# A fused RWKV attention and MLP-mixer kernel: the second down weight in two issues, one batch turned by DMA, two loads held, the last step in two halves of columns

## The chip, the cores and the metric

The kernel runs on one core of one Trainium2 chip. The metric is the device time of one execution in microseconds (us), the median of several runs. The engines are named as in the profile: PE (TensorE, matrix products), DVE (VectorE), ACT (ScalarE), POOL (GpSimd) and SP (SyncE, which here only issues DMAs). PEld is the loading of weights into PE, which overlaps its products.

## The reference

Two stages follow each other. The first is a recurrent attention over 768 positions, for 4 batches of 8 heads of 48 elements; the second is a token mixer and a channel MLP on rows of 384 elements (8 heads times 48).

```python
for t in range(S):                                  # stage 1, per batch and head
    cur = einsum('bhd,bhe->bhde', u * k[t], v[t])
    y[t] = einsum('bhd,bhde->bhe', r[t], state + cur)
    state = w * state + einsum('bhd,bhe->bhde', k[t], v[t])
x = y, heads side by side                           # 4 x 768 x 384
h = (relu(x.T @ w_tok1) @ w_tok2).T                 # token mixing, 768 -> 256 -> 768
u = x + h
out = u + relu(u @ w_ch1) @ w_ch2                   # channel MLP, 384 -> 1536 -> 384
```

## The kernel before

**Units.** The recurrence is computed in chunks of 128 positions. There are 4 batches of 6 chunks, so 24 units, numbered 0 to 23; batch `b` has units `6b` to `6b+5`. A unit loads its rows of k, r and v (three DMAs, tiles `ld_k`, `ld_r`, `ld_v`), scales k and r by powers of the decay (steps `kp`, `rp`, tile `kpr`), casts v (`vb`), turns k and r so that the head's elements lie on the partitions (units 0 to 13 by PE, steps `trk`, `trr`, tile `tr_ps`, copied to `rk`; units 14 to 23 by a DMA transpose `t` straight into `rk`), forms the 128x128 products of each head (`at`, tile `at_ps`), masks them (`AT`), multiplies by v (`y`, tile `y_ps`, with the carried state by `yS`), updates the state (`kv`, `S`) and writes `x_b` (`x`).

**Batches.** When the six chunks of a batch are there, PE computes the token mixer: `hid` (two products for each chunk, `h_ps<-x_b,wtok`), its relu `hr` (tile `h1r`), and `bk`, one step for each chunk (`hT_ps`). DVE adds `x_b` and gives `u_sb` (step `us`, one for each chunk). `u_sb` has to be turned before the channel MLP. Before the change batches 0, 1 and 2 are turned by PE: step `tu` is three transposes of 128x128 into `t_ps`, and ACT or DVE copies them to `uT`. Batch 3 is turned by two DMA transposes on SP's queue, one for each half of three chunks. Then come, for each half of a batch (`sg` 0 and 1), twelve up steps `z` (three products of 128x384 each, `z_ps<-uT,wch`), whose relu `zr` falls to ACT, and for each of its three chunks four down steps `h` (three products each, `h_ps<-wch,zr`). A step is named by batch, half or chunk, and number: `z2_0_0` is the first up step of the first half of batch 2, `h1_5_3` the last down step of chunk 5 of batch 1. The first half of the down steps of a chunk (numbers 0 and 1) reads rows 0 to 5 of twelve of the down weight, the other (2 and 3) rows 6 to 11. `os` adds `u_sb` and the down product on DVE (tile `osb`), and SP writes it out.

**Order.** The kernel holds no order written by hand. `graph` (line 151 on) describes the steps with durations, ranks and dependencies, `Plan.run` places them on the engines by a greedy list schedule, and the instructions are then recorded in the planned order of starts. On the chip each engine, and each DMA queue, works through its instructions in that order, so that one that waits holds up all behind it. Four PSUM buffers (tag `m`) are shared by `tr`, `hid`, `bk`, `tu`, `z` and `h`. All loads, DMA transposes and output writes go through SP's queue. The five weight transfers (which cast to bf16) are issued by POOL, after step `rp5`; the last is `wch2`, the whole down weight, 1152 KB in bf16.

**Names that the change touches.** `weight` in `graph` and in the kernel function issues the weights; the loop at the end of each unit and `load` hold back a unit's first load (`CFG["hold"]`); `pe_turn` names the batches turned by PE, `uTd` is the DMA transpose of half a batch; `parts` cuts the last chunk's down step, `h`, `os_` and `out_`, into halves of columns.

Of the kernel before, what the change touches and what calls it, by code (L numbers as in the profile page):

```python
# [27 lines left out]
NJ = 12  # L28
# [122 lines left out]
def graph(do, cfg):  # L151
# [50 lines left out]
    for u in range(NU):  # L202
# [81 lines left out]
    for b in range(B):  # L284
# [16 lines left out]
        for c in range(C if b not in direct else 0):  # L301
            bk = p.add(f"bk{b}_{c}", [("PE", 2 * MM, 2 * MM + 0.13)], hr + [wx[1]], take=True, rank=r + 0.01 * c, emit=do("bk", b, c))
            us = p.add(f"us{b}_{c}", [DVEP], [bk], give=[f"bk{b}_{c}"], rank=r, emit=do("us", b, c))
            if b in pe_turn:
                t = p.add(f"tu{b}_{c}", [("PE", 0.2, 0.4)], [us], take=True, rank=r + 0.01 * c + 0.005, emit=do("tu", b, c))
                uT.append(p.add(f"uT{b}_{c}", [("ACT", 0.36, 0.53), ("DVE", 0.26, 0.4)], [t], give=[f"tu{b}_{c}"], rank=r, emit=do("uT", b, c)))
            else:
                some.append(us)
                if c % G == G - 1:
                    s = p.add(f"i:uT{b}_{c}", [("SP", 1.35, 1.4)], some, rank=-3000 + c, emit=do("uTd", b, c // G))  # L310
                    uT += [p.transfer(f"x:uT{b}_{c}", s, 1.75, 2.4, 0.0)] * G
                    some = []
        for sg in range(2):
# [7 lines left out]
            for si in range(3):  # L321
# [3 lines left out]
                for part in range(parts):  # L325
                    h, n, mm = None, f"{b}_{c}" + "ab"[part] * (parts > 1), MM / parts + (0.005 if parts > 1 else 0.0)
                    for q in range(4):
                        x = 3 * mm + (own if q == 0 else 0.0)
                        h = p.add(f"h{n}_{q}", [("PE", x, x + 0.13)], zr[3 * q:3 * q + 3] + [wx[3], h], take=(q == 0), rank=m + 0.1 * sg + 0.05 + 0.01 * si + 0.001 * part - (0.02 if q else 0), emit=do("h", b, c, q, part, parts))
# [6 lines left out]
                    stores.append(p.transfer(f"x:o{n}", s, 0.63 / parts, 1.8, 0.0))  # L336
    last = None
# [3 lines left out]
    for s in p.steps:  # L341
        s.rank += cfg.get("rank", {}).get(s.name, 0.0)
# [26 lines left out]
def kernel(  # L369
# [155 lines left out]
    def load(eng, nm, i):  # L525
        b, c = divmod(i, C)
        t = lpool.tile([128, dm], f32, name=f"ld_{nm}")
        ins = sp.dma_start(h3(t), SRC[nm][b, :, ts(c, T), :].rearrange("h s d -> s h d"))
        if i in CFG.get("hold", {}) and nm == CFG.get("lorder", "krv")[0]:
            first = INS[CFG["hold"][i]]  # L530
            tc.add_manual_dep(ins.ins, first.ins.name,
                              mybir.DependencyInfo(mybir.DependencyClass.Sync, mybir.DependencyReason.DATA),
                              reason="weights first")
        loaded[nm, i] = t

    def weight(eng, i):
        t, src = [(wtok1, moe_w_tok1), (wtok2, moe_w_tok2), (wch1, moe_w_ch1), (wch2, moe_w_ch2), (wch1, moe_w_ch1)][i]
        cols = {2: slice(0, dch // 2), 4: slice(dch // 2, dch)}.get(i, slice(None))
        if i == 3 and CFG.get("runs"):
            for f in range(2):  # L540
                half = src[f * dch // 2:(f + 1) * dch // 2]
                pool.dma_start(t[:, f * NJ // 2:(f + 1) * NJ // 2, :], half.rearrange("(p c) k -> p c k", p=128))
        else:
            pool.dma_start(t[:, :, cols], src.rearrange("(c p) k -> p c k", p=128)[:, :, cols])
# [14 lines left out]
    def vb(eng, i):  # L559
        L[i]["vb"] = apool.tile([128, dm], bf16, name="vb")  # L560
        INS["vb", i] = act.copy(L[i]["vb"], loaded["v", i])
# [96 lines left out]
    def y(eng, i):  # L658
        y, first = y_ps(i)
        for a in range(HP):  # L660
            for q in range(2):
                h = 2 * a + q
                INS["y", i] = pe.matmul(y[:, ds(h * D, D)], L[i]["AT"][q][:, a, :], L[i]["vb"][:, ds(h * D, D)],
# [30 lines left out]
    def x(eng, i):  # L694
        b, c = divmod(i, C)
        dve.tensor_add(x_bs[b][:, c, :], L[i]["y"], L[i]["yd"])
# [19 lines left out]
    def bk(eng, b, c):  # L716
        M[b]["bk", c] = psM.tile([128, dm], f32, name="hT_ps", tag="m")
        for i in range(2):
            pe.matmul(M[b]["bk", c], wtok2[:, i, ts(c, 128)], M[b]["h1r"][:, i, :], start=(i == 0), stop=(i == 1))

    def us(eng, b, c):
        dve.tensor_add(M[b]["u"][:, c, :], x_bs[b][:, c, :], M[b]["bk", c])
# [33 lines left out]
    def wch1_j(m, j):  # L756

        if CFG.get("runs"):
            return wch1[:, m].rearrange("p (f q i) -> p f i q", f=2, i=NJ // 2)[:, j // 6, j % 6]
        return wch1[:, m, ts(j, 128)]  # L760

    def z(eng, b, sg, j):
# [3 lines left out]
        for m in range(3):  # L766
            pe.matmul(M[b]["z", sg, j].rearrange("p (c t) -> p c t", c=G), wch1_j(m, j), M[b]["uT"][:, sg * G:sg * G + G, m, :],
# [82 lines left out]
```

## Time and profile before

| | us |
|---|---|
| median of 3 runs | 167.95 |
| their range | 167.8 to 168.52 |
| the profiled execution's own time | 167.91 |
| span in its profile, first to last instruction | 166.2 |

The profile has five parts that are used below: the busy time of each engine, the span in 40 slices, the chain of waits (the chain of work that ended last, followed back from the last instruction), the groups of instructions, and the DMA issues. Beside the page, single views can be asked: the timeline (rows of start, duration, engine, operation, tiles and count, with the idle time before and what ended it in brackets), windows (busy time of every engine in given stretches), who waited for whom, one tile's instructions, and the DMA queues in a window. Matmuls are pipelined: a product of 384 columns has a duration of 326 ns, but the next starts about 163 ns after it.

### The profile page before, as it was taken

What the parts mean: (1) busy time and instruction counts of PE and PEld (TensorE: products, weight loads), DVE (VectorE), ACT (ScalarE), POOL (GpSimd) and SP (SyncE); (2) the same over time, 40 slices, a digit from 0 to 9 for tenths busy, and PEclk for the clock granted to TensorE, in tenths of its full rate; (3) what the DMA queues carried; (4) which work ended last, traced back from release to release, by engine and by line L of the source; (5) the groups of instructions that cost most, each with busy time, mean ns of one, the idle gap of its engine ahead of it and who ended that gap; (6) DMA issues with size and microseconds to landing.
All of it is one profiled execution on the core that took longest, in us unless ns stands there. A gap on an engine that the chain in (4) does not pass through costs nothing.

```text
span 166.2 us, 3805 instructions
## 1 busy us (share of the span) xinstructions
PE 157.5 (95%) x1475; PEld 99.7 (60%) x1475; DVE 100.9 (61%) x206; ACT 85.1 (51%) x172; POOL 80.4 (48%) x97
## 2 busy tenths in 40 slices
PE   6989899996999999999999999999999999999991
PEld 1567665653667666666665666666665565665650
DVE  5499897500288878995599789958967203021021
ACT  3994732797348536698434550457003923905800
POOL 7349680021548869989988789776300000000000
PEclk9999999999999999999999999999999999999999
DMA  5999999999999899998999997993121702102103
GB/s 106 219 224 206 128 147 201 191 184 199 185 216 255 172 221 213 258 205 159 225 210 218 203 190 152 223 239 77 32 99 47 142 0 97 51 0 95 47 29 113
DMA packets 94899, 25.67 MB, mean 154 GB/s; under 512 B 88353, under 2 KB 94882, under 8 KB 94882
## 3 DMA queue, kind: packets, MB, share of 16 engines
q1 hardware_dynamic: 91408, 22.29, 64.1%
q0 software_dynamic: 3472, 3.15, 12.2%
q8 instruction: 11, 0.18, 0.4%
q14 instruction: 6, 0.05, 0.1%
q10 hardware_dynamic: 2, 0.00, 0.0%
HBM read 20.65 MB, written 4.72 MB: 153 GB/s over the span
## 4 chain that ended last, share of the span: by engine, by line
PE 72%; DMA 13%; POOL 4%; ACT 3%; DVE 3%; issue 1%; SPq 1%; POOLq 0%; DVEq 0%; ACTq 0%
PE h_ps L411 30%; PE z_ps L411 21%; DMA wch<-in_moe_w_ch_dram 11%; PE at_ps L411 4%; PE y_ps L411 4%; PE hT_ps L411 4%; PE tr_ps L411 3%; PE kv_ps L411 3%; DMA ld_v<-in_v_dram 2%; ACT rk L411 2%; PE t_ps L411 1%; DVE rku L411 1%; POOL kpr L411 1%; POOL wch L411 1%; POOL yd L411 1%
## 5 line engine op out<-in xcount | busy, mean ns | idle before, releaser
L411 ACT ACTIVATE zr<-z_ps 128x384 bf16<-128x384 f32 x96 | 46.6, 492 | 38.9 <-PE z_ps L411 38.8
L411 PE MATMUL h_ps<-wch,zr 128*128 128x384 bf16 x288 | 55.1, 326 | 1.3 <-DMA wch<-in_moe_w_ch_dram 1.3
L411 PE MATMUL z_ps<-uT,wch 128*128 128x384 bf16 x288 | 53.0, 326 | 0.0
L411 DVE TENSOR_TENSOR osb<-u_sb,h_ps 128x384 f32<-128x384 bf16 x24 | 13.0, 549 | 42.5 <-PE h_ps L411 42.5
L411 PEld LDWEIGHTS <-wch 128*128 128x128 bf16 x288 | 27.2, 98 | 17.0 <-issue 0.2
L411 PEld LDWEIGHTS <-zr 128*128 128x128 bf16 x288 | 26.6, 98 | 17.0 <-DMA wch<-in_moe_w_ch_dram 1.7
L411 DVE TENSOR_TENSOR AT<-at_ps,mask 128x512 bf16<-128x512 f32 x48 | 31.2, 681 | 5.1 <-PE at_ps L411 5.0
L411 POOL TENSOR_TENSOR kpr<-ld_k,wn 128x384 bf16<-128x384 f32 x22 | 22.0, 1000 | 16.0 <-PE z_ps L411 11.4
L411 POOL TENSOR_TENSOR kpr<-ld_r,wp 128x384 bf16<-128x384 f32 x23 | 24.2, 1054 | 6.4 <-DMA ld_r<-in_r_dram 4.4
L411 POOL TENSOR_TENSOR yd<-vb,adg 128x384 f32<-128x384 bf16 x18 | 14.9, 831 | 15.3 <-DVE adg L411 9.5
L411 ACT COPY rk<-tr_ps 128x1024 bf16<-128x1024 bf16 x14 | 14.2, 1013 | 8.9 <-PE tr_ps L411 8.5
L411 PEld LDWEIGHTS <-kpr 128*128 128x128 bf16 x192 | 13.6, 107 | 5.3 <-DVE kpr L411 1.1
L411 DVE TENSOR_TENSOR x_b<-y_ps,yd 128x384 bf16<-128x384 f32 x24 | 13.2, 551 | 3.8 <-PE y_ps L411 3.5
L411 PEld LDWEIGHTS <-rk 48*128 48x128 bf16 (+1 forms) x272 | 10.7, 99 | 7.6 <-ACT rk L411 2.8
L411 ACT CAST vb<-ld_v 128x384 bf16<-128x384 f32 x24 | 12.3, 510 | 2.6 <-DMA ld_v<-in_v_dram 2.6
L411 PE MATMUL tr_ps<-ident,kpr 128*128 128x128 bf16 x112 | 12.3, 244 | 0.4 <-POOL kpr L411 0.2
L411 DVE TENSOR_TENSOR u_sb<-x_b,hT_ps 128x384 bf16<-128x384 bf16 x24 | 12.0, 547 | 1.0 <-PE hT_ps L411 1.0
L411 PE MATMUL h_ps<-x_b,wtok 128*128 128x384 bf16 x48 | 11.3, 326 | 0.1
L411 PE MATMUL at_ps<-rk 48*128 48x128 bf16 x192 | 10.2, 229 | 0.9 <-ACT rk L411 0.8
L411 PEld LDWEIGHTS <-AT 128*128 128x128 bf16 x192 | 8.3, 98 | 3.7 <-DVE AT L411 1.3
L411 PE MATMUL y_ps<-vb,AT 128*128 128x48 bf16 x192 | 9.8, 186 | 0.5 <-DVE AT L411 0.4
L411 PEld LDWEIGHTS <-wtok 128*128 128x128 bf16 x96 | 8.0, 97 | 3.6 <-issue 0.3
(66 smaller groups left out, 132.5 us busy)
## 6 DMA issues: line engine op xcount, KB each, us to landing
ld_k<-in_k_dram SPq DMA_DIRECT2D x24, 192.0 KB, 3.9
ld_r<-in_r_dram SPq DMA_DIRECT2D x24, 192.0 KB, 3.8
ld_v<-in_v_dram SPq DMA_DIRECT2D x24, 192.0 KB, 3.9
out_dram<-osb SPq DMA_DIRECT2D x24, 192.0 KB, 1.9
wch<-in_moe_w_ch_dram POOLq DMA_DIRECT2D x2, 576.0 KB, 9.4
wch<-in_moe_w_ch_dram POOLq DMA_DIRECT2D x1, 1152.0 KB, 18.0
wtok<-in_moe_w_tok_dram POOLq DMA_DIRECT2D x2, 384.0 KB, 5.4
u_bc<-in_u_dram SPq DMA_DIRECT2D x1, 192.0 KB, 4.4
```

Source lines behind the costliest of these rows:

```text
L411: return lambda *args, **kw: tc.keep_in_program_order(f(*args, **kw))
```

## The change

- The down weight `wch2` is fetched in two issues on POOL's queue, rows 0 to 5 (number 3) and then rows 6 to 11 (number 5). Down steps 0 and 1 wait for the first, 2 and 3 for the second.
- `pe_turn` loses batch 2: its 18 transposes on PE and six copies (five on DVE, one on ACT) go, and two DMA transposes on SP's queue take their place.
- The first load of unit 6 is held until the products `y5` are done (before: until the cast `vb5`). The first load of unit 21 is held until `us2_2`, the third sum of batch 2, is done (before: no hold).
- The last down step, chunk 5 of batch 3, is computed in two halves of 192 columns: 24 products of 192 columns instead of 12 of 384, two sums, two writes of 96 KB.
- Paths that no setting used (`runs`, `lorder`) are gone, and settings that stand unused (`xpe`, `off`) came in.

```diff
     def weight(i, after):
-        busy = 1.8 if i == 3 and cfg.get("runs") else 0.9
-        wi[i] = s = p.add(f"i:w{i}", [("POOL", busy, busy + 0.1, True)], after, rank=-50, emit=do("weight", i))
-        took = cfg.get("wtime", (3.0, 2.6, 3.1, 7.7, 3.1))[i]
+        wi[i] = s = p.add(f"i:w{i}", [("POOL", 0.9, 1.0, True)], after, rank=-50, emit=do("weight", i))
+        took = cfg.get("wtime", (3.0, 2.6, 3.1, 7.7, 3.1) if 5 not in cfg["wafter"] else (3.0, 2.6, 3.1, 3.9, 3.1, 3.9))[i]
...
-        for unit, (what, i) in cfg.get("hold", {}).items():
-            if i == u:
-                p.wait(gates[cfg.get("lorder", "krv")[0], unit], [dict(rp=rp, vb=vb, y=y)[what]])
...
-                        h = p.add(f"h{n}_{q}", [("PE", x, x + 0.13)], zr[3 * q:3 * q + 3] + [wx[3], h], take=(q == 0), rank=m + 0.1 * sg + 0.05 + 0.01 * si + 0.001 * part - (0.02 if q else 0), emit=do("h", b, c, q, part, parts))
+                        h = p.add(f"h{n}_{q}", [("PE", x, x + 0.13)], zr[3 * q:3 * q + 3] + [wx[3] if q < 2 else wx.get(5, wx[3]), h], take=(q == 0), rank=m + 0.1 * sg + 0.05 + 0.01 * si + 0.001 * part - (0.02 if q else 0), emit=do("h", b, c, q, part, parts))
...
+    for unit, what in cfg.get("hold", {}).items():
+        p.wait(gates["k", unit], [next(s for s in p.steps if s.name == "".join(map(str, what)))])
...
-    + [("w", 0), ("w", 1), ("w", 2), ("w", 4), ("w", 3)],
-    wafter={0: "x:v4", 1: "rp5", 2: "rp5", 4: "rp5", 3: "rp5"},
+    + [("w", 0), ("w", 1), ("w", 2), ("w", 4), ("w", 3), ("w", 5)],
+    wafter={0: "x:v4", 1: "rp5", 2: "rp5", 4: "rp5", 3: "rp5", 5: "rp5"},
     slack={"v5": 3.0},
-    hold={6: ("vb", 5)},
+    hold={6: ("y", 5), 21: ("us", "2_2")},
...
-    pe_turn=(0, 1, 2),
+    pe_turn=(0, 1),
...
+    parts=2,
...
+        rows = {3: slice(0, NJ // 2), 5: slice(NJ // 2, NJ)}.get(i, slice(None)) if 5 in CFG["wafter"] else slice(None)
+        pool.dma_start(t[:, rows, cols], src.rearrange("(c p) k -> p c k", p=128)[:, rows, cols])
```

Because the planner places everything anew, the order of instructions changes far from the edits too. Both programs, built, have these orders at the places that are spoken of below (steps of one engine, from left to right):

```text
PE, first down steps
  before  z0_0_0 ... z0_0_11, z0_1_0 ... z0_1_6, h0_0_0, h0_1_0, h0_0_1, h0_1_1, h0_0_2, ...
  after   z0_0_0 ... z0_0_11, h0_0_0, h0_1_0, h0_0_1, h0_1_1, h0_2_0, z0_1_0, h0_2_1, h0_0_2, ...
PE, batch 1 turned
  before  bk1_0, y12, bk1_1, bk1_2, tu1_0, at13, kv13, yS13, tu1_1, bk1_3, tu1_2, bk1_4, bk1_5, tu1_3, pg13, z1_0_0, tu1_4
  after   kv13, bk1_0, bk1_1, y12, bk1_2, at13, tu1_0, yS13, tu1_1, bk1_3, tu1_2, bk1_4, bk1_5, pg13, z1_0_0, tu1_3, kv14, tu1_4
DVE, at the same place
  before  AT_12, AT_12, us1_0, x12, us1_1, us1_2, pr13, ...  (S13 comes after us1_5)
  after   adg12, AT_12, AT_12, S13, us1_0, x12, us1_1, us1_2, pr13, ...
PE, batch 2 turned
  before  y18, bk2_0, bk2_1, h1_3_3, h1_4_1, tu2_0, tu2_1, kv20, h1_4_2, bk2_2, bk2_3, bk2_4, at19, tu2_2, ... z2_0_0
  after   y18, bk2_0, bk2_1, h1_3_3, kv20, bk2_2, at19, bk2_3, bk2_4, bk2_5, yS19, h1_4_2, h1_5_0, h1_4_3, h1_5_1,
          h1_5_2, y19, at20, h1_5_3, z2_0_0, yS20, z2_0_1, z2_0_2, z2_0_3, y20, ...
SP's queue
  before  t18, o1_2, k20, r20, v20, t19, k21, r21, v21, k22, r22, v22, k23, t20, o1_3, r23, v23, t21, o1_4, t22, o1_5, t23
  after   k20, t18, o1_2, r20, v20, t19, t20, o1_3, uT2 (first half), uT2 (second half), k21, o1_4, r21, v21, k22, o1_5,
          r22, v22, k23, r23, v23, t21, t22, o2_0, o2_1, t23, o2_2, uT3 (first half), ...
PE, after z2_0_0
  before  at21 behind h2_0_0, at22 and at23 among h2_0 and h2_1, bk3_0 to bk3_5 before z2_1_2
  after   z2_0_0 to z2_0_11, fourteen down and up steps, kv21 and kv22, at21, at22 among z2_1_5 and z2_1_6, at23 behind z2_1_8, then
          bk3_2, h2_3_3, bk3_3, bk3_4, h2_4_1, bk3_5, h2_4_2, h2_5_0, h2_4_3, h2_5_1, h2_5_2, z3_0_0
```

(`o` is the write of a chunk's output, `k`, `r`, `v` the loads, `t` the DMA transpose of a unit, `pg` and `adg` small steps of a unit, `pr` a product on DVE.)

More of the change, by code (lines that the diff above doesn't have):

```diff
@@ L341, in graph @@
     for s in p.steps:
[L342 removed]
+        s.rank += cfg.get("rank", {}).get(s.name, 0.0) + cfg.get("off", {}).get(s.name.rstrip("0123456789").rstrip("_"), 0.0)
     rng = random.Random(cfg.get("seed", 0))
@@ L536, in weight @@
     def weight(eng, i):
-        t, src = [(wtok1, moe_w_tok1), (wtok2, moe_w_tok2), (wch1, moe_w_ch1), (wch2, moe_w_ch2), (wch1, moe_w_ch1)][i]
+        t, src = [(wtok1, moe_w_tok1), (wtok2, moe_w_tok2), (wch1, moe_w_ch1), (wch2, moe_w_ch2), (wch1, moe_w_ch1), (wch2, moe_w_ch2)][i]
         cols = {2: slice(0, dch // 2), 4: slice(dch // 2, dch)}.get(i, slice(None))
[L539 to L544, printed above, removed]
+        rows = {3: slice(0, NJ // 2), 5: slice(NJ // 2, NJ)}.get(i, slice(None)) if 5 in CFG["wafter"] else slice(None)
+        pool.dma_start(t[:, rows, cols], src.rearrange("(c p) k -> p c k", p=128)[:, rows, cols])
     def gd(eng):
```

31 lines of the change are left out of this document (17 added, 14 removed).

## The prediction

> **What bounds the kernel now.** I read the windows first: the span cut where PE starts or stops, each row with the stretch, its length, and the busy time of PE, PEld, DVE, ACT and POOL. Then the view of who PE waited for.
>
> ```profile
> 39.83:41.17 1.34, 0.00 (x1) 0.01 (x1) 0.00 (x0) 0.53 (x2) 0.16 (x1) 1.00 1.26 250
> 41.17:70.00 28.83, 28.69 (x362) 19.33 (x364) 21.28 (x44) 15.21 (x29) 21.42 (x24) 1.00 1.01 214
> 70.00:100.00 30.00, 29.73 (x300) 18.72 (x297) 24.40 (x43) 17.59 (x40) 26.57 (x29) 1.00 1.02 204
> 100.00:130.00 30.00, 29.97 (x279) 18.80 (x278) 24.64 (x50) 9.74 (x21) 14.02 (x15) 1.00 0.54 121
> 130.00:162.74 32.74, 32.69 (x202) 19.47 (x199) 4.25 (x9) 15.69 (x33) 0.00 (x0) 1.00 0.22 64
> 162.74:166.20 3.46, 0.00 (x0) 0.00 (x0) 0.54 (x1) 0.00 (x0) 0.00 (x0) 1.00 0.17 62
> ```
> ```profile
> PE h_ps L411 <- DMA wch<-in_moe_w_ch_dram: 1.3, 1, 1.3
> ```
>
> From 41.17 to 162.74 PE is idle for 0.49 us in all, at the full clock (1.00). So the end is set by when PE can start at 41.17, by the PE work behind that, and by 3.46 us of tail. Time on another engine counts only where PE then waits for it.
>
> **1. The down weight in two issues, unit 6 held.** The timeline of PE around the one large stall, the chain of waits, the landing times of the three `wch` issues, and queue 0 (the weights: packets, MB, share) in the stretches 24 to 27, 28 to 31 and 32 to 39:
>
> ```profile
> 31.38 8.45 PE L411 MATMUL z_ps<-uT,wch 128*128 128x384 bf16 x51
> 41.17 2.61 PE L411 MATMUL h_ps<-wch,zr 128*128 128x384 bf16 x15 [1.34 <-DMA wch<-in_moe_w_ch_dram]
> ```
> ```profile
> 21.63 1.50 POOL wch L411 x2
> 23.13 17.99 DMA wch<-in_moe_w_ch_dram
> ```
> ```profile
> DMA to landing us min/median/max: 8.1/10.7/18.0
> ```
> ```profile
> q0 software_dynamic: 391, 0.58, 113.5%
> ```
> ```profile
> q0 software_dynamic: 354, 0.52, 95.1%
> ```
> ```profile
> q0 software_dynamic: 1344, 1.04, 93.8%
> ```
>
> Issues at 21.63, 22.38 and 23.13 landed at 29.73, 33.08 and 41.12. The last brings 1152 KB (1.18 MB) in 8.04 us, 147 GB/s, which is the queue's own rate there (1.04 MB in 7 us). In two issues the first half should land near 33.1 + 4.0 = 37.1, the second where the whole did, unless the queue gets faster. A step of three products takes 0.49 us (8.45 less 0.16 of pipeline, over 51 products), and 31.38 is the start of `z0_0_2`, so `z0_0_11` ends at 36.26. In the new order `h0_0_0` is next: it waits to about 37.1 (0.8), runs seven steps that need only the first half (3.4), and `h0_0_2` waits from 40.5 for the second half. In the old order too, 19 steps stand between `z0_0_0` and the stall. So PE goes on at the second half's landing with the same 19 steps done as before: the split alone cuts the stall in two pieces and gains nothing. A gain needs an earlier landing.
>
> That can come from the hold. Loads of unit 6 ran beside the weights:
>
> ```profile
> 23.33 0.37 SPq L411 DMA_DIRECT2D ld_k<-in_k_dram  x1
> 23.74 0.70 SPq L411 DMA_DIRECT2D ld_r<-in_r_dram  x1
> ```
> ```profile
> 24.85 0.41 PE L411 MATMUL y_ps<-vb,AT 128*128 128x48 bf16 x8
> ```
> ```profile
> ld_r<-in_r_dram SPq DMA_DIRECT2D x1, 192.0 KB, 17.1
> ```
>
> `y5` ends at 25.26, so the load moves from 23.33 to about 25.3, 2.0 us. Before the loads flow the weights get 0.58 MB in 3 us (193 GB/s), beside them 173. Two more microseconds at the higher rate are 0.04 MB, which at 147 GB/s is 0.27 us. I take -0.25; bounds 0 and, if all bytes of the loads beside the weights (173 against 193) were spared for all the 8 us, -0.8. One issue more on POOL costs 0.75 there (1.50 for two) with nothing behind it until unit 6 comes. Behind the held load SP's whole queue waits, and POOL (`kp6`, `rp6`) and `trk6` wait for that: `ld_r` of unit 6 landed at 40.84; 2.0 later and 1.0 on POOL gives 43.9, and `trr6` now stands eight steps and a transpose behind the second half, past 44.5. Covered by 0.6; without it, one for one.
>
> The Trainium skill, in "DMA: Bandwidth & Descriptors", section "Anatomy of one DMA — SWDGE (gpsimd) path", fits a DMA as a fixed 2.0 us plus its bytes at 436 GB/s. If a fixed part were paid in series, the split would cost it again; that is rival E. By that rule E would be 2.0 us, but the trace speaks for overlap.
>
> **2. Batch 2 turned by DMA.** The chain of waits in that stretch, and the steps around:
>
> ```profile
> 101.56 0.33 PE t_ps L411 x6
> ...
> 103.52 0.33 PE at_ps L411 x8
> 103.85 0.27 PE t_ps L411 x3
> ...
> 104.16 0.34 PE t_ps L411 x3
> ...
> 126.50 1.95 PE hT_ps L411 x12
> ```
>
> Twelve of the 18 transposes stand here with 0.94, six of them at 0.33 without a wait; the last six at that pace 0.33. Removed from PE: 1.27 (0.99 of work, 0.28 of waits for `u_sb`). The copies to `uT` go from DVE and ACT, which gains nothing more.
>
> What comes instead: is the DMA hidden? DVE's row gives 0.47 for one sum after another, and the DMA rows give 3.4 for the two of batch 3 in a quiet queue and 3.1/3.8/5.4 (least, median, most) for the ten unit turns:
>
> ```profile
> 126.86 2.88 DVE L411 TENSOR_TENSOR u_sb<-x_b,hT_ps 128x384 bf16<-128x384 bf16 x6 [0.26 <-PE hT_ps L411]
> ```
> ```profile
> uT<-u_sb SPq DMA_TRANSPOSE x2, 3.4
> ```
> ```profile
> DMA to landing us min/median/max: 3.1/3.8/5.4
> ```
>
> From the start of `bk2_0` DVE has `x18`, `us2_0`, `us2_1`, `os1_3`, `us2_2`: the last ends at about 2.5, and SP issues the DMA at 2.6. PE meanwhile has five `bk` beside `bk2_0` (0.16 a product: 1.95 in all), seven steps of 0.49 (3.4), two `at` of 0.33, and `kv`, `yS`, `y` at up to 0.2: it reaches `z2_0_0` at 6.6. So the DMA has 4.0. At 3.4 to 3.8 nothing is late; at 5.4 PE waits 1.4. Loads are held and the queue is quiet, as for batch 3, so I take 0. Batch 3 moves as well: from the end of `bk3_2` PE has seven steps and three `bk`, 4.4; the sum takes 0.55, so its DMA has 3.7, and 3.4 was measured in the same quiet state. 0 again, up to 1.7 at 5.4.
>
> **3. Units 21 to 23.** The hold puts their loads behind both transposes on SP.
>
> ```profile
> 96.07 0.58 SPq L411 DMA_DIRECT2D ld_k<-in_k_dram  x1
> ```
> ```profile
> 115.77 0.33 PE at_ps L411 x8
> ```
>
> The first was issued at 96.07, now at about 106, while `at21` (115.77) moves only to 26 steps behind `z2_0_0`, about 120. From `k21`: nine loads at 0.70 (the row at 23.74) and two writes are out after 7 us, and `kp`, `ku`, `rp` on POOL end at about the same time (3.9 to land, three at 1.0); `t21` lands 3.8 to 5.4 later, at 117 to 119. Covered by 1 to 3 us; I take 0.
>
> **4. Batch 1 in another order.** No edit, but a cost: DVE now does `S13` before `us1_0`, one operation of 0.47 ahead of the chain `us1`, `tu1`, `uT1`, on which PE waited already before (the first row). And `z1_0_0` goes ahead of `tu1_3`, so it takes one of four PSUM buffers until its relu on ACT (second row, 0.49) frees it for a transpose.
>
> ```profile
> 72.32 0.56 DVE u_sb L411
> ```
> ```profile
> L411 ACT ACTIVATE zr<-z_ps 128x384 bf16<-128x384 f32 x96 | 46.6, 492 | 38.9 <-PE z_ps L411 38.8
> ```
>
> Bounds 0 (PE has other steps) and 0.96 (both in full); I take +0.7, near the upper end, since few unit steps are left to fill.
>
> **5. The last step in halves.** The chain's last piece, writes, queue 1 from 163 to 166, and transposes of 128 columns:
>
> ```profile
> 44.49 0.22 PE tr_ps L411 x4
> ```
> ```profile
> 162.72 0.55 DVE osb L411
> ```
> ```profile
> out_dram<-osb SPq DMA_DIRECT2D x24, 192.0 KB, 1.9
> ```
> ```profile
> q1 hardware_dynamic: 144, 0.20, 18.4%
> ```
> ```profile
> L411 DVE TENSOR_TENSOR AT<-at_ps,mask 128x512 bf16<-128x512 f32 x48 | 31.2, 681 | 5.1 <-PE at_ps L411 5.0
> ```
>
> 128 columns with new weights each take 55 ns, so 192 columns at 81 are not bound by the loads, and 24 of them take what 12 of 384 took: 0. The Trainium skill, "TensorE: Matmul & The Clock Gate", section "Back-to-back issue gap", gives 81 ns for 128 columns and 131 for 512; a straight line (an estimate) puts 192 at 87, 0.14 more for the 24, against the trace's 55.
>
> A sum of 512 elements takes 681 ns, of 384 549 (0.55): 1.0 ns an element, so the last half ends 0.2 earlier. Of the write, the engines were busy for 18.4% of about 3 us, 0.55; half is at most 0.28, part of it lost to the two issues in a row. I take -0.1. Together -0.3, bounds 0 and -0.48.
>
> **The sum.** -0.25 - 1.27 + 0 + 0 + 0.7 - 0.3 = -1.1. Against the profiled execution's 167.91 (span 166.2 and 1.7 around it; 0.04 below the median of the runs): 166.8, rounded up to **166.9** for small waits.
>
> **The rivals.**
> - A, as summed: 166.2 to 167.6. 0.55.
> - B, the new order gives it back: with transposes gone, PE meets at the same places the chains of DVE and POOL (busy 24.40 and 26.57 of 30 us from 70 to 100), the waits of part 4 recur in batches 2 and 3, and 0.96 there and as much in batch 2 leave 168.0. For it: these two engines are nearly full. Against: from 100 on both have room. 0.22.
> - C, slower: the DMA turns are late. Place: `z2_0_0` and `z3_0_0`, which PE cannot pass. Price: one for one beyond 4.0 and 3.7 from issue to landing. At 4.4 the two waits eat the 1.1 gained, at 4.8 they cost 1.9 (168.8), at 5.4 3.1 (170.0). For it: the unit turns' 5.4. Against: 3.4 twice in a quiet queue. 0.12.
> - D, larger gain: the weights come 0.8 earlier with the loads kept off, and the write and the waits of part 4 are at their better ends: about 165.7 to 166.2. Against: the loads come only 2 us later and then share the engines as before. 0.08.
> - E, the change doesn't do what it says, as the second issue pays a fixed time in the queue: PE goes on later by up to the 1.9 that a small write takes: 168.8. Against: the two halves of the up weight landed 3.35 apart with 576 KB (0.59 MB), 176 GB/s, the queue's rate without a gap. 0.03.
>
> **How the numbers follow.** A measurement of this kernel can tell about 0.5% from no change, 0.84 us: below 167.11 is faster, above 168.79 slower. Faster: 0.42 of A and D, 0.50. Same: 0.13 of A, 0.20 of B, 0.02 of C, 0.01 of E, 0.36. Slower: 0.10 of C, 0.02 of B, 0.02 of E, 0.14. The range 165.8 to 168.6 leaves out the late end of C and the outer ends of B, D and E.
>
> **What would show it.** Two PE waits on `wch`, near 36.3 and 40.5, that sum to about 1.1, with `h0_0_2` at 40.9 (a later one is E, an earlier one D); no PE wait on the `uT` DMA above 0.3 at about 105 and 135 (else C); waits near 70 to 74 grown by 0.7 (part 4); `at21` without a wait; the last sum at 0.35 and the end 0.3 sooner behind PE. A wait on a load of unit 6, or on `kpr` between 115 and 125, would prove parts 1 or 3 wrong.

## The result, and the profile after

The changed kernel took 167.0 us (median of 10 runs, 166.38 to 167.5), the kernel before beside it 167.88: a ratio of 0.9936, 95% interval 0.9915 to 0.9957. That is 0.9 to 1.1 us less; 166.9 was predicted. A second comparison (experiment 5) gave 0.9965 (0.9931 to 0.9999). Single slow runs, over 1.5% above the fastest of their kernel (one in experiment 8, a few of the kernel before), are left out of medians and ratios.

The profiled execution of the changed kernel took 166.97 us, its span is 165.0. In both the granted clock is 1.00 from 31 us to the end of PE's work. Cut where the path changes hands, the two profiled executions differ like this:

| piece of the path, us | before | after | difference | in the sum |
|---|---|---|---|---|
| start to the step that waits for the whole down weight | 41.17 | 40.84 | -0.33 | -0.25 |
| from there to the end of PE's last columns | 121.35 | 120.38 | -0.97 | -1.27 + 0.7 |
| from there to the end of the span | 3.68 | 3.79 | +0.11 | -0.3 |
| span | 166.20 | 165.01 | -1.19 | -1.1 |

So the total came out as summed, while the last two terms did not. The end of PE's last columns is the start of its last product and the time its columns take (0.16 for 384, 0.08 for 192): 162.52 and 161.22.

**The weight.** Who PE waited for from 31 us on, in the changed kernel (us in total, times, longest):

```profile
PE h_ps L411 <- ACT zr L411: 0.6, 1, 0.6
PE h_ps L411 <- DMA wch<-in_moe_w_ch_dram: 0.5, 1, 0.5
PE t_ps L411 <- ACT uT L411: 0.4, 1, 0.4
PE t_ps L411 <- DVE uT L411: 0.2, 1, 0.2
```

The first two rows are the two pieces of the old stall of 1.3. (The first is put down to a relu; its step starts at 36.77, and the first half of the weight landed at 36.72.) The tile view of `wch` and the first load of unit 6:

```profile
L411 POOL DMA_DIRECT2D wch<-in_moe_w_ch_dram x4: 768/808/862, 21.2 to 23.6; - x4
...
DMA to landing us min/median/max: 8.2/12.4/17.2
```
```profile
25.19 0.37 SPq L411 DMA_DIRECT2D ld_k<-in_k_dram  x1
```

The last of the four issues, at 23.60, landed 17.2 later, at 40.79 (41.12 before). But the first weight issue was 0.38 earlier too (21.25 for 21.63). Counted from it the last landing is at 19.54, before the change 19.49: in this execution the gain of 0.33 came from a quicker start and not from the hold.

**The idle time of PE.** From the starts of all matmuls I took how much later each began than the columns of the one before it need (0.423 ns a column, 0.1625 us for 384), and added it up by stretches (net: where two products overlap, the difference is negative):

| stretch, us | 41-66 | 66-76 | 76-97 | 97-110 | 110-138 | 138-end | sum |
|---|---|---|---|---|---|---|---|
| before | 1.27 | 1.00 | 0.68 | 0.50 | 0.34 | 0.00 | 3.79 |
| after | 1.15 | 1.94 | 0.28 | 0.23 | 0.16 | 0.03 | 3.79 |

The sums are equal: what PE lost in batch 1 it got back in small pieces elsewhere, and the 0.97 is the work of the 18 transposes (0.99). The windows show the same at a coarser grain (stretch, its length, busy time of PE, PEld, DVE, ACT, POOL), first before, then after:

```profile
66.00:76.00 10.00, 9.88 (x116) 6.42 (x115) 9.46 (x20) 7.77 (x19) 8.96 (x11) 1.00 1.05 226
76.00:97.00 21.00, 20.80 (x197) 12.84 (x196) 16.38 (x27) 10.93 (x25) 18.34 (x19) 1.00 1.04 205
```
```profile
66.00:76.00 10.00, 9.24 (x110) 6.15 (x109) 9.61 (x22) 6.00 (x14) 7.95 (x10) 1.00 1.01 205
76.00:97.00 21.00, 21.00 (x203) 13.03 (x202) 15.97 (x29) 10.92 (x26) 20.17 (x21) 1.00 1.09 211
```

The timeline of the changed kernel around the waits of PE in batch 1:

```profile
70.18 0.48 ACT L411 COPY uT<-t_ps 128x384 bf16<-128x384 bf16 x1 [0.96 <-PE t_ps L411]
...
70.71 0.33 PE L411 MATMUL t_ps<-ident,u_sb 128*128 128x128 bf16 x3 [0.37 <-ACT uT L411]
...
71.08 0.97 ACT L411 COPY uT<-t_ps 128x384 bf16<-128x384 bf16 x2 [0.42 <-PE t_ps L411]
...
71.61 0.81 PE L411 MATMUL hT_ps<-h1r,wtok 128*128 128x384 bf16 x4
...
71.74 1.47 DVE L411 TENSOR_TENSOR u_sb<-x_b,hT_ps 128x384 bf16<-128x384 bf16 x3
...
73.05 0.49 ACT L411 ACTIVATE zr<-z_ps 128x384 bf16<-128x384 f32 x1 [0.34 <-PE z_ps L411]
73.21 0.36 DVE L411 COPY uT<-t_ps 128x384 bf16<-128x384 bf16 x1
...
73.59 0.33 PE L411 MATMUL t_ps<-ident,u_sb 128*128 128x128 bf16 x3 [0.24 <-DVE uT L411]
```

Counted as in the table, PE loses 0.53 before 70.71, 0.24 before 71.61 and 0.40 before 73.59; the kernel before loses 0.08 and 0.22 among its transposes. All three are waits for a PSUM buffer, and the built program says for which:

- `tu1_1` (70.71) takes the buffer of `tu1_0` and waits for its copy on ACT, which ends at 70.66. Before the change that buffer goes to `bk1_3`, behind three unit steps.
- `bk1_4` (71.61) waits in the same way for the copy of `tu1_1`, the first of the two at 71.08, which ends at 71.56.
- `tu1_4` (73.59) takes the buffer of `z1_0_0` and waits for its relu on ACT, which ends at 73.54. The row names DVE's copy, because that ended last, at 73.57; but the program does not wait for that copy there.

It is buffers and not `S13` that are late: `tu1_0` itself starts without a wait.

**The turn by DMA.** The tile view of `uT` from 95 to 140:

```profile
L411 SPq DMA_TRANSPOSE uT<-u_sb x4: 1249/1286/1321, 103.1 to 135.7; - x4
...
DMA to landing us min/median/max: 3.2/3.3/3.4
```

All four turns took 3.2 to 3.4, and no row of the waits names them. The first of batch 2 was issued at 103.06 and landed at 106.45, and `z2_0_0` started at 107.19; for batch 3 the three times are 133.70, 136.93 and 137.30.

**The tail**, in the timeline:

```profile
160.81 0.58 PE L411 MATMUL h_ps<-wch,zr 128*128 128x192 bf16 x5
...
161.17 0.72 DVE L411 TENSOR_TENSOR osb<-u_sb,h_ps 128x192 f32<-128x192 bf16 x2 [1.18 <-PE h_ps L411]
161.55 0.81 SPq L411 DMA_DIRECT2D out_dram<-osb  x2
```

One sum of 192 columns takes 0.35 as predicted. But there are two in a row behind PE, since PE makes the halves in turn, three products each, so that the first is ready only three products ahead of the second. From the end of PE's columns to the last issue (161.98) it is 0.76, before 0.78. And from that issue to the end it is 3.03, before 2.90, though the write is half as long.

### The profile page after: what moved, and what is told of

Its sections match the earlier page's. It is cut to its first block, busy times and chain, and to the rows that moved or that the text cites. A ratio compares the mean times of both kernels' runs of the same rounds, so it can differ in the third digit from the quotient of the medians.

```text
span 165.0 us, 3803 instructions
## 1 busy us (share of the span) xinstructions
PE 155.1 (94%) x1469; PEld 98.7 (60%) x1469; DVE 101.1 (61%) x204; ACT 82.5 (50%) x168; POOL 82.3 (50%) x99
## 4 chain that ended last, share of the span: by engine, by line
PE 73%; DMA 13%; ACT 4%; POOL 3%; SPq 2%; DVE 2%; issue 1%
PE h_ps L411 30%; PE z_ps L411 24%; DMA wch<-in_moe_w_ch_dram 10%; PE y_ps L411 5%; PE at_ps L411 4%; PE hT_ps L411 3%; PE tr_ps L411 3%; PE kv_ps L411 3%; SPq L411 2%; DMA ld_v<-in_v_dram 2%; ACT rk L411 2%; POOL wch L411 1%; DVE u_sb L411 1%; POOL kpr L411 1%; ACT S L411 1%
## 5 line engine op out<-in xcount | busy, mean ns | idle before, releaser
L411 ACT ACTIVATE zr<-z_ps 128x384 bf16<-128x384 f32 x96 | 46.1, 493 | 46.8 <-PE z_ps L411 46.6
L411 PE MATMUL h_ps<-wch,zr 128*128 128x384 bf16 (+1 forms) x300 | 54.1, 320 | 1.1 <-ACT zr L411 0.6
L411 PE MATMUL z_ps<-uT,wch 128*128 128x384 bf16 x288 | 54.0, 326 | 0.0
L411 PEld LDWEIGHTS <-zr 128*128 128x128 bf16 x300 | 27.9, 98 | 17.3 <-DMA wch<-in_moe_w_ch_dram 1.0
L411 PEld LDWEIGHTS <-wch 128*128 128x128 bf16 x288 | 27.0, 98 | 16.2
L411 DVE TENSOR_TENSOR AT<-at_ps,mask 128x512 bf16<-128x512 f32 x48 | 31.0, 682 | 7.1 <-PE at_ps L411 7.1
L411 DVE TENSOR_TENSOR osb<-u_sb,h_ps 128x384 f32<-128x384 bf16 (+1 forms) x25 | 13.2, 536 | 36.1 <-PE h_ps L411 36.0
L411 POOL TENSOR_TENSOR kpr<-ld_k,wn 128x384 bf16<-128x384 f32 x22 | 22.6, 1027 | 18.5 <-DMA ld_k<-in_k_dram 13.2
L411 POOL TENSOR_TENSOR kpr<-ld_r,wp 128x384 bf16<-128x384 f32 x23 | 23.2, 1011 | 6.7 <-DMA ld_r<-in_r_dram 3.6
L411 POOL TENSOR_TENSOR yd<-vb,adg 128x384 f32<-128x384 bf16 x18 | 15.1, 843 | 16.2 <-DVE adg L411 10.8
L411 ACT COPY rk<-tr_ps 128x1024 bf16<-128x1024 bf16 x14 | 14.2, 1011 | 6.7 <-PE tr_ps L411 6.6
L411 DVE TENSOR_TENSOR x_b<-y_ps,yd 128x384 bf16<-128x384 f32 x24 | 13.3, 553 | 5.6 <-PE y_ps L411 5.3
L411 PEld LDWEIGHTS <-kpr 128*128 128x128 bf16 x192 | 12.9, 103 | 4.9 <-POOL kpr L411 1.1
L411 PEld LDWEIGHTS <-rk 48*128 48x128 bf16 (+1 forms) x272 | 10.4, 97 | 7.6 <-ACT rk L411 2.5
L411 ACT CAST vb<-ld_v 128x384 bf16<-128x384 f32 x24 | 12.3, 511 | 3.3 <-DMA ld_v<-in_v_dram 3.2
L411 DVE TENSOR_TENSOR u_sb<-x_b,hT_ps 128x384 bf16<-128x384 bf16 x24 | 12.2, 548 | 1.3 <-PE hT_ps L411 1.2
L411 PE MATMUL tr_ps<-ident,kpr 128*128 128x128 bf16 x112 | 11.9, 234 | 0.6 <-POOL kpr L411 0.6
L411 PE MATMUL h_ps<-x_b,wtok 128*128 128x384 bf16 x48 | 11.4, 326 | 0.2 <-DMA wtok<-in_moe_w_tok_dram 0.2
L411 PEld LDWEIGHTS <-AT 128*128 128x128 bf16 x192 | 8.4, 98 | 4.0 <-DVE AT L411 1.7
L411 PEld LDWEIGHTS <-wtok 128*128 128x128 bf16 x96 | 8.0, 97 | 4.3 <-issue 0.7
L411 PE MATMUL at_ps<-rk 48*128 48x128 bf16 x192 | 9.8, 222 | 0.9 <-ACT rk L411 0.9
L411 PE MATMUL y_ps<-vb,AT 128*128 128x48 bf16 x192 | 9.6, 186 | 1.0 <-DVE AT L411 0.9
```

The costliest lines, as they stand in the source:

```text
L411: return lambda *args, **kw: tc.keep_in_program_order(f(*args, **kw))
```

## The experiments

Twelve runs in groups of four (1 to 4, 5 to 8, 9 to 12), each group on one chip with the kernel before beside it. The edits are to the changed kernel.

**1. The down weight in one issue, planned anew.**

```diff
-    + [("w", 0), ("w", 1), ("w", 2), ("w", 4), ("w", 3), ("w", 5)],
-    wafter={0: "x:v4", 1: "rp5", 2: "rp5", 4: "rp5", 3: "rp5", 5: "rp5"},
+    + [("w", 0), ("w", 1), ("w", 2), ("w", 4), ("w", 3)],
+    wafter={0: "x:v4", 1: "rp5", 2: "rp5", 4: "rp5", 3: "rp5"},
```

> The down weight comes in one issue again and the order is planned anew; the held loads, the turn by DMA and the halves stay. The theory (the split by itself gains nothing, and the order planned around it costs the idle time of PE seen in batch 1, about 0.9 us): 166.0 us, 0.6 % below the changed kernel; one wait of PE of about 1.0 us on the weight near 40, its landing at 40.6 to 40.8 (the place where the second half lands now); between 66 and 76 us PE idles 1.0 us as before the change and not 1.9. Rival 1 (the split is what gains): 167.2 to 167.5, the weight landing at 41.1. Rival 2 (the idle time of batch 1 comes from elsewhere in the new order): 167.0, with 1.9 us idle between 66 and 76.

Measured: 166.99 us, ratio 0.9922 (0.9889 to 0.9955). Idle between 66 and 76: 0.91, as the theory said, so the 0.94 belong to the order that is planned around the split. The time is not what the theory said; by the intervals it cannot be told from the changed kernel's. The profiled execution was the slowest of this kernel (168.24): PE came late to the weight, which landed at 40.48, and did not wait; then it waited twice for late transfers (in the first row the cast had itself waited for a load of v), and idled 2.35 between 76 and 97:

```profile
PE kv_ps L411 <- ACT vb L411: 0.8, 1, 0.8
PE at_ps L411 <- DMA rk<-kpr: 0.8, 1, 0.8
```

Whether that is this kernel or this execution was left to experiment 6.

**2. One issue, the order of the split.**

```diff
     def weight(eng, i):
+        if i == 5:
+            return
...
-        rows = {3: slice(0, NJ // 2), 5: slice(NJ // 2, NJ)}.get(i, slice(None)) if 5 in CFG["wafter"] else slice(None)
+        rows = slice(None)
```

> The order of the changed kernel's steps stays, but the fourth weight issue brings the whole down weight and the fifth is left out. The theory (with the second half ordered late, 12 steps of the first half's columns stand behind the weight, so the order needs the first half early): the weight lands at 40.6 to 40.8, the first product of the down weight waits from 36.3 to there, 4.3 us in place of 0.8, the second wait goes, so the end comes 3.3 to 3.4 us later: 170.2 to 170.5. Rival (a weight in one issue lands earlier, because an issue has a fixed part): landing at 39 to 39.5, time 168.7 to 169.2.

Measured (one time): 169.62, 2.65 above the changed kernel's profiled execution. Both sizes missed. The weight landed at 40.05, earlier than the theory had it, and the first down product waited for it:

```profile
PE h_ps L411 <- DMA wch<-in_moe_w_ch_dram: 2.0, 1, 2.0
```

The structure held: the down steps start at 40.09, seven steps later (3.41) they are where the changed kernel is at 40.84, 2.66 behind it. That PE came to the stall only at 37.97 made the wait short, not the end early. Nor does one issue land sooner: it is 18.66 behind the first weight issue here, and two issues with the same hold (experiment 9) are at 18.79.

**3. Batch 2 turned by PE.**

```diff
-    hold={6: ("y", 5), 21: ("us", "2_2")},
+    hold={6: ("y", 5)},
...
-    pe_turn=(0, 1),
+    pe_turn=(0, 1, 2),
```

> Batch 2 is turned by PE again and units 21 to 23 are not held; the weight in two issues, the hold of unit 6 and the halves stay. The theory (18 transposes cost 0.99 us on PE and their waits 0.28, and nothing covers them): 168.2 to 168.6, 0.8 to 1.0 % above the changed kernel. Rival B (DVE and POOL set the pace in batches 1 and 2, so that the transposes lie in time in which PE would wait anyway): 167.0 to 167.4.

Measured: 167.89, ratio 0.9978 (0.9948 to 1.0008); that is 0.4% above the changed kernel's ratio (0.9936, measured apart from it), half of what was expected; the intervals allow up to 0.9%. The profiles are clearer. The page's rows for PE, after the change and here:

```profile
PE 155.1 (94%) x1469; PEld 98.7 (60%) x1469; DVE 101.1 (61%) x204; ACT 82.5 (50%) x168; POOL 82.3 (50%) x99
```
```profile
PE 158.1 (95%) x1487; PEld 101.7 (61%) x1487; DVE 100.7 (61%) x206; ACT 85.3 (51%) x173; POOL 81.1 (49%) x98
```

From the whole weight (41.07) to the end of PE's columns (162.66) it is 121.59, in the changed kernel 120.38: the turn on PE costs 1.21, 0.21 of it more idle time between 97 and 110. Rival B falls: the transposes are not hidden.

**4. Unit 6 held to the earlier point.**

```diff
-    hold={6: ("y", 5), 21: ("us", "2_2")},
+    hold={6: ("vb", 5), 21: ("us", "2_2")},
```

> Unit 6 is held only to its earlier point, as before the change, all else as in the changed kernel. The theory (the hold alone brings the weights earlier, 0.25 to 0.3 us): the second half lands at 41.05 to 41.1, the two waits on the weight sum to 1.35 us, time 167.2 to 167.3. Rival 1 (the split alone brings it): landing at 40.8 as in the changed kernel, 167.0. Rival 2 (the hold is worth more, since first half and second half both profit): landing at 41.5, 167.7.

Measured: 167.37, ratio 0.9942 (0.9909 to 0.9976), which cannot be told from the changed kernel. The second half landed at 41.66, 19.82 behind the first weight issue; PE idled 1.56 for the two halves. Nearest to rival 2, but one landing says little beside a start that moves by more than a microsecond from one execution to the next. It counts as one point of the row in experiment 10.

**5. The changed kernel again.**

> The changed kernel as it is, a second time, on the chip of the next three, so that they can be compared with it. What it is to settle: whether the 0.9 us of idle time of PE between 66 and 76 us and the end of the tail (last write issued 3.0 us ahead of the end, where the kernel before has 2.9 for a write of twice the size) are the kernel's or one execution's. The theory (both are the kernel's): idle 1.9 us in that stretch again, 3.0 us again. Rival (one execution's): 1.0 to 1.4 us idle, 2.6 us. Time against the kernel before: ratio 0.992 to 0.996.

Measured: 167.47, ratio 0.9965 (0.9931 to 0.9999). Idle between 66 and 76: 1.94 again; last issue to end: 3.03 again. Both are the kernel's.

**6. One issue, and the load of u on POOL's queue.** The edit of experiment 1 and:

```diff
-        sp.dma_start(u_bc, u.rearrange("h d -> (h d)")[None, :].to_broadcast([128, dm]))
+        pool.dma_start(u_bc, u.rearrange("h d -> (h d)")[None, :].to_broadcast([128, dm]))
```

> The down weight in one issue, planned anew, and the load of u put on POOL's queue instead of SP's, so that each later transfer of SP takes the semaphore of the one before it. The theory (the order without the split saves 0.9 us in batch 1; in the first profile of it that was eaten by late loads and a late unit turn, 0.8 us each, which one execution shows and not the median; the shift saves 0.4 us of the waits at the end): 165.9 to 166.2 on a chip where the changed kernel has 167.1. Rival 1 (the loads of units 15 to 17 are the next bound, so that the 0.9 us comes back as waits on them in every execution): idle of 2 us or more between 76 and 97 us again, 166.7. Rival 2 (the semaphore's place is worth nothing): 0.4 more than either.

Measured: 166.63, ratio 0.9891 (0.9859 to 0.9922), 0.84 below the changed kernel on the same chip. The profile has no wait on loads, nor have those of experiments 11 and 12, while one of the kind stands in experiment 4, in the order of the split; so the waits of experiment 1 go with the execution and not with the one issue:

```profile
PE h_ps L411 <- DMA wch<-in_moe_w_ch_dram: 1.1, 1, 1.1
PE tr_ps L411 <- POOL kpr L411: 0.3, 1, 0.3
PE kv_ps L411 <- POOL ku L411: 0.2, 1, 0.2
```

From the whole weight (40.72) to the end of PE's columns it is 120.00, 0.38 less than with the split, although POOL's extra issue costs 0.3 of it. The theory's 0.9 for the order was too much: 76 to 97 gives 0.65 idle here where the order of the split has 0.28.

**7. The load of u on POOL's queue alone** (the second edit of experiment 6).

> The changed kernel with the load of u on POOL's queue instead of SP's and nothing else. SP's transfers take eight semaphores in turn, and at the end SP waits for them in the order of their numbers; the changed kernel's last write has the lowest one, so that seven more waits of 0.06 us come behind its landing. The theory (the place of the semaphore): the last write takes the highest one, SP goes from its landing to the end without the seven waits, from the issue of the last write to the end 2.5 to 2.6 us in place of 3.0, time 0.4 us below the changed kernel. Rival (the landing itself is later in the changed kernel, whatever the semaphore): 3.0 us again, the same time. POOL pays 0.8 us for the issue; PE waits for POOL no more than before.

Measured: 167.17, ratio 0.9952 (0.9925 to 0.9979). The last write is issued at 162.90 and the span ends at 165.50, 2.60 later, as the theory said; the changed kernel has 3.03 in both its executions. SP's semaphore instructions at the end, from the trace:

```
changed kernel                        u on POOL's queue
161.98 last write issued              162.90 last write issued
163.68 wait ended by its landing      163.33 to 163.71 seven waits
163.74 to 164.11 seven more waits     164.11 wait ended by the write before
164.18 drain                          164.60 wait ended by its landing
165.01 end                            164.66 drain
                                      165.50 end
```

Eight semaphores go round among SP's transfers and ACT's, and at the end SP waits for them in the order of their numbers, 0.06 us each. Which one the last write gets is decided by the count of transfers before it. The kernel before had two waits behind the landing, the changed kernel has seven, this one none. In the time little of it is left (0.3 below experiment 5's, within the intervals), for another reason: PE waited 0.4 for POOL (`PE tr_ps L411 <- POOL kpr L411: 0.4`), behind the issue. From this kernel experiment 6 differs by the one issue and its order alone: 166.63 against 167.17, ratios 0.9891 against 0.9952, so these are worth 0.5 to 1 us.

**8. Units 21 to 23 not held.**

```diff
-    hold={6: ("y", 5), 21: ("us", "2_2")},
+    hold={6: ("y", 5)},
```

> Units 21 to 23 are not held, so that their loads stand ahead of the two DMA transposes of batch 2 on SP, all else as in the changed kernel. The theory (the DMA turn is hidden only because the queue in front of it is kept clear): both transposes are issued 2 to 3 us later, or take 4.5 to 5.4 us beside the loads; PE waits 1.5 to 3 us at the first up step of batch 2, near 110, time 168.5 to 170. Rival (the transposes have room enough either way, and the hold does nothing): no wait above 0.3 us there, time as the changed kernel.

Measured: 169.72 (7 runs), ratio 1.0098 (1.0055 to 1.014): the time of the theory. Who PE waited for, and SP's queue:

```profile
PE at_ps L411 <- DMA rk<-kpr: 1.0, 1, 1.0
PE z_ps L411 <- DMA uT<-u_sb: 0.6, 1, 0.6
```
```profile
103.85 1.76 SPq L411 DMA_TRANSPOSE rk<-kpr  x1
105.71 2.82 SPq L411 DMA_TRANSPOSE uT<-u_sb  x2
```

The turn itself takes no longer (3.3 to 3.5), it is issued 2.6 later (105.71 for 103.06), behind loads and a unit turn. The wait at the up step is 0.6, less than the theory's 1.5, and the unit turn costs the other 1.0. So the place of rival C is right, but not its cause, a longer transfer. The turn by DMA loses without the hold of unit 21.

**9. The halves one after the other.** The diff is to the last step's plan:

```diff
-                        h = p.add(f"h{n}_{q}", [("PE", x, x + 0.13)], zr[3 * q:3 * q + 3] + [wx[3] if q < 2 else wx.get(5, wx[3]), h], take=(q == 0), rank=m + 0.1 * sg + 0.05 + 0.01 * si + 0.001 * part - (0.02 if q else 0), emit=do("h", b, c, q, part, parts))
+                        h = p.add(f"h{n}_{q}", [("PE", x, x + (0.13 if parts == 1 or q == 3 else 0.0))], zr[3 * q:3 * q + 3] + [wx[3] if q < 2 else wx.get(5, wx[3]), h], take=(q == 0), rank=m + 0.1 * sg + 0.05 + 0.01 * si + 0.05 * part - (0.02 if q else 0), emit=do("h", b, c, q, part, parts))
```

> The two halves of the last down step run one after the other (12 products of the first half, then 12 of the second) instead of three by three in turn; all else as in the changed kernel, the place of the last semaphore too. The theory (in the changed kernel the first half's sum waits for PE nearly to its end, so both sums stand behind PE): the first sum now runs beside the second half's products, about 0.6 us ahead of PE's end, and from the end of PE's last product to the issue of the last write it takes 0.40 us in place of 0.76; the time falls by 0.35 us. Rival (the second write cannot follow sooner, because SP takes 0.43 us from one issue to the next and the second sum is not what it waits for): 0.7 us again, the same time.

Measured: 166.85, ratio 0.9956 (0.9932 to 0.998), between the two ratios of the changed kernel: no gain that can be told. From the end of PE's columns (161.96) to the last issue (162.66) it is 0.70, the rival's number, but neither reason. The timeline:

```profile
161.18 0.35 DVE L411 TENSOR_TENSOR osb<-u_sb,h_ps 128x192 f32<-128x192 bf16 x1 [0.44 <-PE h_ps L411]
162.28 0.35 DVE L411 TENSOR_TENSOR osb<-u_sb,h_ps 128x192 f32<-128x192 bf16 x1 [0.74 <-DMA out_dram<-osb]
```

The first sum now ends 0.4 ahead of PE. The second has its product at 161.96 and starts at 162.28: `osb` has three buffers, and in the built program this sum waits for the write of the third sum before it to land. A fourth buffer was not tried.

**10. Unit 6 held longer.**

```diff
-    hold={6: ("y", 5), 21: ("us", "2_2")},
+    hold={6: ("us", "0_5"), 21: ("us", "2_2")},
```

> Unit 6 is held 4 to 5 us longer, to the last sum of batch 0, all else as in the changed kernel. Over the executions so far, the time from the first weight issue to the last landing falls by about 0.27 us for each us that the load of unit 6 is issued later: 19.5 and 19.8 at 1.7 and 2.6 us behind the first weight issue, 18.7 at 5.6. Theory (the loads cost the weights their share of the engines for as long as they run beside them): at 8 us behind it 17.9 to 18.2, so that the second half lands about 39.5, PE goes on 1.2 us sooner, time 165.8 to 166.1. Rival 1 (the estimate of the prediction, half that slope, 0.135 a us): 18.5, landing near 40.2, 166.5. Rival 2 (unit 6 comes too late for PE): a wait of PE on its loads or on what is made of them behind 42, and 167 or more.

Measured: 166.15 (4 runs), ratio 0.9891 (0.985 to 0.9931), where the kernel of experiment 9, which differs from the changed one in the last step alone, has 0.9956 on the same chip. The tile view of `wch` and the held load:

```profile
L411 POOL DMA_DIRECT2D wch<-in_moe_w_ch_dram x4: 758/800/855, 21.9 to 24.2; - x4
...
DMA to landing us min/median/max: 8.0/10.9/15.0
```
```profile
32.01 0.37 SPq L411 DMA_DIRECT2D ld_k<-in_k_dram  x1
```

The hold was longer than expected, 10.1 us behind the first weight issue, and the second half landed 17.37 behind it. With the other executions, in us behind the first weight issue:

| load of unit 6 issued | 1.7 (before) | 2.6 (exp. 4) | 3.7 to 5.6 (ten executions) | 9.2 (exp. 12) | 10.1 (exp. 10) |
|---|---|---|---|---|---|
| last weight landed | 19.49 | 19.82 | 18.66 to 19.55, mean 19.15 | 18.06 | 17.37 |

That is 0.25 for each us of hold (19.49 to 17.37 over 8.4), nearly twice the prediction's 0.135. It is an estimate from the two ends: executions with much the same hold differ by 0.5, so a step of 2 us cannot be told from one of them. What of the loads delays the weights was not separated. Rival 2 falls: unit 6 landed at 39.7 to 41.0, and PE did not wait for it. In this execution PE did not wait for the weight either, so the start of PE had become the bound. It did not wait in the profiled execution of experiment 9 too, so that these two profiles do not show where the 0.7 of the medians comes from; experiment 12 does.

**11. Together: one issue, halves in a row, u behind the weights on POOL's queue.** The edits of experiments 1 and 9, and the load of u issued in `weight` behind the last weight:

```diff
+        if i == 3:
+            pool.dma_start(u_bc, u.rearrange("h d -> (h d)")[None, :].to_broadcast([128, dm]))
```

> Together what has paid so far: the down weight in one issue and the order planned anew, the halves in a row, and the load of u on POOL's queue, here right behind the weights and not at its old place, where PE waited 0.3 to 0.5 us for POOL behind it. The theory (the parts add up: 0.6 from the order of batch 1 and what follows it, 0.4 from the semaphore, 0.35 from the halves): 1.3 us below the changed kernel, ratio to the kernel before 0.986 to 0.988. Rival (the loads are the next bound between 60 and 100 us, and u beside the loads of unit 6 delays those): 0.990 or more, with waits on loads or unit turns of 0.8 us.

Measured: 165.88 (6 runs), ratio 0.9899 (0.987 to 0.9929): the median nearer to the rival's number, not by its mechanism. No wait on loads is there, and batch 1 is as before the change:

```profile
66.00:76.00 10.00, 9.88 (x117) 6.38 (x114) 9.23 (x19) 7.81 (x19) 8.97 (x11) 1.00 1.03 219
76.00:97.00 21.00, 20.79 (x196) 12.73 (x194) 16.62 (x27) 10.87 (x24) 18.20 (x20) 1.00 1.11 208
```

From the whole weight (40.92) to the end of PE's columns it is 119.92, 0.46 less than in the changed kernel; from there to the end 3.22, 0.57 less. The sum, 1.0, is less than the 1.3 expected because the halves gave 0.07 in place of 0.35.

**12. The same, with unit 6 held longer** (the edit of experiment 10 as well).

> The last kernel with unit 6 held to the last sum of batch 0 as well. The theory of the hold: another 0.5 to 1.2 us, ratio to the kernel before 0.979 to 0.984. Rival (unit 6 late): waits of PE behind 42, no gain on the last kernel or a loss.

Measured: 165.01 (4 runs), ratio 0.984 (0.9815 to 0.9865). From 31 us on the view lists a single wait of PE, for POOL:

```profile
PE kv_ps L411 <- POOL ku L411: 0.2, 1, 0.2
```

Against experiment 11 PE goes on with the whole weight at 40.23 in place of 40.92, although the first weight was issued 0.7 later (22.12 for 21.41); this 0.69 is all by which the span is shorter (163.38 for 164.06). This version beats both kernels: 2.7 us below the kernel before.

## Why the prediction was right, and where it was not

**The sum held because two errors cancelled, which is luck.** Behind the whole weight PE gained 0.97 where -1.27 and +0.7 make -0.57, and the tail lost 0.11 where -0.3 stood: 0.40 too little in one place, 0.41 too much in the other.

**1. Split and hold (-0.25).** The split by itself: right. The last landing behind the first weight issue is 19.15 in the mean of ten executions with the same hold, some with one issue (18.98, 18.66, 19.35, 19.47) and some with two (18.79 to 19.55); so no fixed time is paid and none is saved, and E falls. The Trainium skill's fixed 2.0 us for each DMA ("DMA: Bandwidth & Descriptors", section "Anatomy of one DMA — SWDGE (gpsimd) path") would put the second half 2.0 later if it were paid in series; the runs disagree with that reading of it, as the trace of before did. The two waits are where they were predicted, up to 36.77 and 40.84, and 1.1 in sum by the view; and the second half is used from 40.84 (40.9 predicted). The hold is mis-sized: the term used 193 against 173 GB/s for the 2 us moved, 0.27; by the measured slope 2 us of hold would be 0.5. The profiled execution does not show even the 0.25 (19.54 at a hold of 3.9, 19.49 at 1.7); its 0.33 are those of a quicker start. The start differs by up to 1.3 us between executions (first weight issue 21.25 to 22.59), which is why a single pair of profiles can't size this term.

**2. Batch 2 by DMA (-1.27).** Right: 0.99 of work gone, 0.27 of idle time between 97 and 110, and experiment 3 gives 1.21 for putting it back. The turns took 3.4 and 3.35, and 3.24 in batch 3, against budgets of 4.0 and 3.7. So `z2_0_0` stood 4.1 behind the issue and `z3_0_0` 3.6, and the turns had 0.7 and 0.4 to spare. C did not come, and experiment 8 shows that this hangs on the hold of unit 21.

**3. Units 21 to 23 (0).** Right: `at21` to `at23` wait for nothing.

**4. Batch 1 in another order (+0.7).** In its place the loss was larger, 0.94, and near the upper bound of 0.96. That it is the order's is shown: 1.85 to 2.2 us of idle time in all nine executions of the split's order, 0.9 to 1.0 in the four with one issue. But the step took the loss for the whole effect of the new order. Between 76 and 97 the same order saves 0.4 (before the change PE waits there 0.2 for POOL's `ku`), and 0.3 more came in small pieces from 41 to 66 and from 110 on. Against the kernel before that leaves +0.3 (0.97 gained of 1.27), not +0.7; against the same change with one issue it costs 0.4 to 0.5 (experiments 6 and 11; it is 1.0 between 7 and 6, which both have u on POOL's queue). Of the two causes named, one is there: the buffer that `z1_0_0` holds until its relu costs 0.40 (0.49 was its price). `S13` costs nothing. The other two waits, 0.53 and 0.24, are for buffers of the transposes themselves, because fewer unit steps now stand between them; the prediction had no such term, so that its 0.7 came near by a cause that it had only in part. None of these was changed by itself. Rival B, that these waits recur in batch 2, is refuted by the idle time there (0.23 from 97 to 110). The argument given against B did not hold as it stood: in the row from 100 to 130 DVE is busy for 24.64 of 30, no less than before 100; the room on DVE lies behind 110.

**5. The last step in halves (-0.3).** This step failed: +0.11. "The last half ends 0.2 earlier" reckoned with one sum behind PE, and the halves are made in turn, so there are two; the sums so gained 0.02 in place of 0.2. Made in a row, the halves gain no more, because the three `osb` buffers hold the second sum back (experiment 9). The write itself is 0.18 shorter (1.68 in experiment 7, 1.86 before), more than the 0.1 taken. And the end has five more waits of 0.06 behind the last landing than before, 0.3, because the two transfers of the turned batch and the extra write shift the round of semaphores (experiment 7); no step of the prediction looked there. PE's own cost is 0 as said: the 24 products start 82.5 ns apart (159.24 to 161.14). The estimate from the Trainium skill's figures ("TensorE: Matmul & The Clock Gate", section "Back-to-back issue gap") was 87, where a straight line through 81 and 131 gives 89; the trace is nearer to half of 163.

## What to carry to other kernels

A split or a move changes a planned order far from its place: compare the idle time of the critical engine stretch by stretch, and price the order apart from the edit. When a transfer ends the longest stall, look first at what else moves bytes while it runs; holding one unit's loads 5 to 6 us longer than the change does brought 0.7 to 0.9 us here (experiments 10 and 12), while the split and the halved write brought nothing. When the view names what a wait was for, and two candidates end within 0.05 us, read in the program what the instruction waits for. A shorter last piece helps only if nothing is queued between it and the end: the sum beside it, the buffer it needs, and the waits behind its landing.

## What the runs showed of the hardware that was not expected

- At the end of the kernel SP waits for every transfer semaphore in turn, 0.06 us each. One transfer more or less on SP's queue moves the last write's place in that row: from the wait that its landing ended to the end it took 0.90 us with none behind it (experiment 7), 1.03 with two (before), 1.33 with seven (after).
- The weights landed about 0.25 us later for each us by which the loads beside them started earlier (19.49 at 1.7 us behind the first weight issue, 17.37 at 10.1), an estimate from the table of experiment 10.
- The DMA turns of batches 2 and 3 took 3.2 to 3.5 also where loads stood around them (experiment 8); what was late there was their issue.
- The start varies: from the first instruction to the first weight issue 21.25 to 22.59 us in the profiles, the changed kernel itself with 21.25 and 22.59. Five of the thirteen executions behind the change did not wait for the weight at all.
